# An attention laid out as 64 partitions x 9 tokens, multiplied in 64x64 quadrants, ahead of two expert layers

## The chip, the core and the metric

The kernel runs on one core of one Trainium2 chip. The metric is the device time of one execution in microseconds (us), lower is better; a kernel's time is the median over its runs. A profile is one execution of its own, taken by the hardware profiler, with its own time. Engines: PE is the matrix engine (PEld its weight loads), DVE, ACT and POOL work on tiles, SP issues most DMAs, and 16 DMA engines move the data.

## The reference, cut to what matters

Attention without softmax over 8 batches, 8 heads, 576 tokens and 64 features, a root-mean-square norm per head, then two mixture-of-experts layers over the 4608 tokens. All inputs are fp32.

```python
kv = np.einsum('bhsd,bhse->bhde', k, v)          # 64 x 64 for each batch and head
out = np.einsum('bhsd,bhde->bhse', q, kv)
rms = np.sqrt(np.mean(out * out, axis=-1, keepdims=True) + 1e-06)
x = out / rms * g_norm                           # then rows of 8 heads x 64 = 512, 4608 tokens
# first layer: logits x @ w_gate + log1p(exp(x @ w_noise)) * noise, two best of 8 experts,
#   softmax over the two, sum of relu(x @ w1[e]) @ w2[e]
# second layer: tokens with x @ w_skip > 0 go to the best of 8 experts and are added to
```

## The kernel before

One program, in two phases.

**The attention phase** reads q, k and v, multiplies, normalises, computes the gate logits, and writes rows of 512 features (as two fp16 halves, high and low part, in the bytes of 512 fp32) to `xrows` in HBM, with 16 numbers of routing behind each row. Its work is written out by hand as steps. `subs` (L791) lists 56 of them: for each pair of batches `pb`, 2 x 6 steps of main tokens and 2 of left-over tokens. In step i the loop of L828 runs slot 0 of what is due, transposes the queries of step i+2 (`q_transposed`, L453), runs slot 1, makes the output of step i (`out_sub`, L475), and runs slot 2. Everything else is placed by `at(step, f, slot)`: the tables `KV`, `GC`, `FIN`, `ROUTE`, `WSTEPS`, `EPLAN` and `CLEAR` at the top of the file give the steps. ACT, DVE, POOL and SP take their instructions in just this order (`manual_schedule`, L292), as PE does throughout.

- Loads (L318 to L336). The 576 tokens of a head are 512 main tokens, 4 on each of 128 partitions, and 64 left-over ones. k and v come in half batches (4 heads, 1 KB per partition and head), q in quarters (2 of the 4 tokens of a partition, 512 B runs), the left-over tokens of two batches together (256 B runs).
- Key-value products (`kv_half`, L407): for each head two 128x128x128 products on pairs of tokens (L416), of whose four 64x64 blocks the two on the diagonal are wanted, then one for the left-over tokens of two heads (L421). ACT and DVE add the two blocks (L424, L426), and POOL and ACT copy the sum into both diagonal blocks of `kvbd` (L315 runs what is due), a block-diagonal 128x128 matrix with 32 columns behind it.
- Gate columns (`gate_columns`, L437): key-value times gate weights goes into these 32 columns (L442 to L451), so that the output product gives the logits too.
- Output (`out_sub`): for each head and pair of tokens one 128x160 product with `kvbd` (L481); the left-over tokens use 64-column halves of the array (L487, L488). An eviction (L490 on ACT or L492 on DVE, by the letters of `OSBE`) brings three heads from the bank to `osb`; a square (L495 on ACT, L497 on POOL, by `SQE`) and a sum (L501, DVE) follow a step later.
- `finish` (L504) places, one to six steps later, the inverse root (L517 to L521, L146 to L148), the normalisation (L525, POOL), the logits (L546, L549), the high part (L529, ACT), the low part (L532, DVE) and the write of the rows (`rows_out`, L703, SP).
- `route_half` (L553) chooses the experts of half of the tokens (four batches), mostly on DVE, in 27 pieces; for the first half they are placed between later steps by `ROUTE`, for the second they come in the tail (`TAIL`, L856) together with four early tiles of expert 0 (`early_tile`, L732). In between lie the splitting of expert 0's weights into fp16 halves (L173, L190, L191), and nine DMAs that clear the output (`clear`, L814).

PSUM has 8 banks: pool `pA` 3 (transposes, first expert layer), `pB` 2 (outputs, second layer), `pS` 2 (small), `pK` 1 (key-value).

**The expert phase** (L876 on) gathers rows of `xrows` by expert and runs both expert layers (L232 and L271 are their products). The change leaves it alone, but for the names of the PSUM pools.

## Time and profile before

| | |
|---|---|
| median of 3 runs | 1272.91 us (1269.75 to 1274.32) |
| the profiled execution | 1278.91 us, its span 1276.7 us |
| PE busy | 1184.7 us, 93% of the span |
| DVE, ACT, POOL busy | 823.3, 664.9, 372.5 us (64, 52, 29%) |
| DMA | 293 MB, mean 230 GB/s |

The span runs from the first instruction to the last; times inside it count from its start. A busy share is an average over both phases, which have different limits, so it is read by stretch. Each row of the sections below is a whole line of the profile or of an answer of the trace. In groups of instructions, "out<-in shapes xcount | busy us, mean ns | idle before" gives first the operation and its tiles, then the time in which at least one of them ran, the mean of one, and the engine's idle time just before them with what ended it. "64*128" on PE is rows by columns of the array in use. An fp32 product is recorded as two instructions, an fp32 transpose as one.

### The profile page before, as it was taken

What the parts mean: (1) busy time and instruction counts of PE and PEld (TensorE: products, weight loads), DVE (VectorE), ACT (ScalarE), POOL (GpSimd) and SP (SyncE); (2) the same over time, 40 slices, a digit from 0 to 9 for tenths busy, and PEclk for the clock granted to TensorE, in tenths of its full rate; (3) what the DMA queues carried; (4) which work ended last, traced back from release to release, by engine and by line L of the source; (5) the groups of instructions that cost most, each with busy time, mean ns of one, the idle gap of its engine ahead of it and who ended that gap; (6) DMA issues with size and microseconds to landing.
All of it is one profiled execution on the core that took longest, in us unless ns stands there. A gap on an engine that the chain in (4) does not pass through costs nothing.

```text
span 1276.7 us, 25310 instructions
## 1 busy us (share of the span) xinstructions
PE 1184.7 (93%) x9341; PEld 845.6 (66%) x9341; DVE 823.3 (64%) x3034; ACT 664.9 (52%) x1209; POOL 372.5 (29%) x454
## 2 busy tenths in 40 slices
PE   5868779999999999999999999999899899999996
PEld 5767667767676767676767666676657565666664
DVE  1667887526586877787778877787867665333321
ACT  2578663156664765675667776576754231122210
POOL 2223242202323333324232323233232231312220
PEclk8979789999999999999999999999999999999998
DMA  9999984748996989699799999999995664786570
GB/s 239 291 238 295 320 226 107 180 137 244 297 246 181 232 254 243 190 246 313 132 308 270 289 301 287 255 251 277 276 311 150 141 209 121 221 289 192 155 261 16
DMA packets 311409, 293.33 MB, mean 230 GB/s; under 512 B 205022, under 2 KB 256222, under 8 KB 307180
## 3 DMA queue, kind: packets, MB, share of 16 engines
q1 hardware_dynamic: 288316, 208.22, 62.6%
q0 software_dynamic: 22384, 82.36, 18.7%
q8 instruction: 75, 1.23, 0.4%
q10 hardware_dynamic: 576, 1.05, 0.3%
q14 instruction: 58, 0.48, 0.1%
HBM read 172.86 MB, written 93.42 MB: 209 GB/s over the span
## 4 chain that ended last, share of the span: by engine, by line
PE 62%; issue 12%; DVE 9%; ACT 6%; DMA 6%; POOL 3%; SPq 1%; POOLq 0%; DVEq 0%; ACTq 0%
PE b L271 29%; PE a L232 26%; DMA x2T<-xh 2%; PE b L481 1%; PE kvps L416 1%; ACT wjunk L173 1%; DMA vm<-in_v_dram 1%; DMA x2Tr<-xh 1%; POOL out_dram L1190 1%; DVE xh L933 1%; DMA yo<-ydram,gi 1%; DVE wb L191 1%; ACT wb L190 1%; DVE x L532 1%; PE a L463 1%
## 5 line engine op out<-in xcount | busy, mean ns | idle before, releaser
L232 PEld LDWEIGHTS <-wa 128*128 128x128 f16 x5184 | 460.8, 99 | 52.7 <-issue 4.7
L232 PE MATMUL a<-xT,wa 128*128 128x256 f16 (+6 forms) x3648 | 390.4, 268 | 2.0 <-DMA xT<-xg 1.1
L271 PE MATMUL b<-wb,hh 128*128 128x512 f16 x1488 | 338.8, 380 | 9.9 <-ACT hh L240 9.8
L271 PEld LDWEIGHTS <-hh 128*128 128x128 f16 x1488 | 141.3, 98 | 169.3 <-ACT hh L240 13.9
L240 ACT ACTIVATE hh<-a 128x512 f16<-128x512 f32 (+5 forms) x186 | 107.2, 579 | 199.9 <-PE a L232 193.7
L271 PE MATMUL b<-wb,hl 128*128 128x512 f16 x744 | 176.2, 380 | 0.0
L241 DVE SCALAR_TENSOR_TENSOR hl<-a,hh 128x512 f16<-128x512 f32 (+5 forms) x186 | 124.5, 674 | 72.5 <-ACT hh L240 72.4
L1049 POOL DMA_INDIRECT xg<-xrows,idxp x67 | 65.4, 976 | 320.6 <-DVE orow L1073 279.7
L271 PEld LDWEIGHTS <-hl 128*128 128x128 f16 x744 | 72.9, 98 | 88.6 <-issue 1.1
L1103 ACT ACTIVATE ysb<-b,gate 128x512 f32<-128x512 f32 x73 | 49.7, 681 | 118.5 <-PE b L271 104.4
L232 PE MATMUL a<-x2Tr,wa 128*128 128x256 f16 (+1 forms) x1152 | 107.4, 255 | 1.9 <-DMA x2Tr<-xh 1.9
L1111 POOL DMA_INDIRECT out_dram<-x,oi x67 | 68.2, 1018 | 139.5 <-DVE pi L1019 57.1
L173 ACT ACTIVATE wjunk<-stage 128x1024 bf16<-128x1024 f32 x96 | 101.3, 1055 | 2.1
L191 DVE SCALAR_TENSOR_TENSOR presplit<-stage,wscl,presplit 128x1024 f16<-128x1024 f32 x64 | 80.5, 1278 | 15.8 <-ACT presplit L190 14.9
L1082 POOL DMA_INDIRECT yo<-ydram,gi x67 | 71.2, 1062 | 55.2 <-DMA x2T<-xh 17.7
L190 ACT ACTIVATE presplit<-stage,wscl 128x1024 f16<-128x1024 f32 x64 | 71.2, 1140 | 19.6 <-DVE wscl L183 19.6
L481 PE MATMUL b<-kvbd,qTs 128*128 128x160 f32 x256 | 52.8, 346 | 21.8 <-issue 10.0
L929 ACT ACTIVATE jk<-x 128x512 bf16<-128x512 f32 x67 | 42.1, 629 | 58.3 <-DVE x L1107 57.9
L1107 DVE TENSOR_TENSOR x<-ysb,yo 128x512 f32<-128x512 f32 x67 | 46.3, 691 | 25.2 <-ACT ysb L1103 18.4
L525 POOL TENSOR_TENSOR osb<-osb,rinv 128x1024 f32<-128x1024 f32 (+1 forms) x20 | 37.1, 1854 | 86.9 <-DVE rinv L148 71.3
L932 ACT ACTIVATE xh<-x,x2ss 128x512 f16<-128x512 f32 x67 | 45.4, 714 | 31.7 <-DVE x2ss L139 31.7
L481 PEld LDWEIGHTS b<-kvbd,qTs 128*128 128x128 f32 x256 | 42.6, 219 | 26.5 <-issue 10.9
(356 smaller groups left out, 1534.7 us busy)
## 6 DMA issues: line engine op xcount, KB each, us to landing
stage<-in_moe_w_dram SPq DMA_DIRECT2D x32, 2048.0 KB, 10.9
wsd<-presplit SPq DMA_DIRECT2D x8, 2056.0 KB, 9.3
ydram<-ysb SPq DMA_DIRECT2D x64, 256.0 KB, 7.9
wsd<-presplit SPq DMA_DIRECT2D x8, 2048.0 KB, 7.5
out_dram<-zeros SPq DMA_DIRECT2D x9, 1024.0 KB, 8.2
km<-in_k_dram SPq DMA_DIRECT2D x16, 512.0 KB
vm<-in_v_dram SPq DMA_DIRECT2D x16, 512.0 KB, 8.1
qm<-in_q_dram SPq DMA_DIRECT2D x16, 512.0 KB, 6.8
```

What stands on the lines that cost most here:

```text
L173: A.activation(junk, st[:, F * c:F * c + F], AF.Square, accum_out=acc[:, c:c + 1], **kw)
L190: A.activation(hi[:, d], st[:, d], AF.Copy, scale=sc)
L191: V.scalar_tensor_tensor(lo[:, d], st[:, d], sc, hi[:, d], op0=ALU.mult, op1=ALU.subtract)
L232: PE.matmul(ps[:, i, :], a[:, c, fs], xT[:, b + c, 0:nt], start=(n == 0), stop=(n == 11))
L240: behind[0] = A.activation(hh[:, fsl, 0:nt], ps, AF.Relu).ins
L241: i = V.scalar_tensor_tensor(hl[:, fsl, 0:nt], ps, 0.0, hh[:, fsl, 0:nt], op0=ALU.max, op1=ALU.subtract)
L271: PE.matmul(ps, a[:, f, gsl], b[:, f, :], start=(fs.start == 0 and i == 0), stop=(fs.stop == 8 and a is hl and f == 7))
L481: PE.matmul(po[:, i, :], qT[:, i, :], kvb[b % 4][:, h0 + i, :], start=True, stop=True)
L1049: G.indirect_dma_start(out=xg[:, g], out_offset=None, in_=xrows, in_offset=bass.IndirectOffsetOnAxis(ap=idx[:, t0 + g:t0 + g + 1], axis=0))
L1082: G.indirect_dma_start(out=yo, out_offset=None, in_=ydram[0:BASE[e], :], in_offset=bass.IndirectOffsetOnAxis(ap=gi[:, g:g + 1], axis=0), b ...
L1103: A.activation(ysb, ps, AF.Copy, scale=gate[:, g:g + 1])
L1111: s = G.indirect_dma_start(out=out, out_offset=bass.IndirectOffsetOnAxis(ap=oi[:, g:g + 1], axis=0), in_=x2[:, g], in_offset=None, bounds_ ...
```

## The change

A sequence of 576 tokens is laid out as 64 partitions x 9 tokens, and two heads of it fill the 128 partitions: partition 64c + p, tokens 9p to 9p+8 of head 2h+c. So there are no left-over tokens, and a load of two heads is one stretch of HBM with 2304 bytes to a partition. A pair of batches is the unit (`NP` = 4); k, v and q come in half batches (4 heads) of both batches of the pair.

- Key-value products are 64x64x64 in quadrants: row half by head c, column half by batch bl, 9 tokens added up in PSUM; two banks, one for each c. They come in four parts (`KVAT`) 8 to 5 steps before the pair's first output; `kv_out` evicts them (DVE and ACT), and POOL copies each to the other partition half; no block-diagonal matrix is left.
- Queries are transposed as 128x128 still, for two heads and two neighbouring tokens; after it the partition half is the token.
- Output products are 64x64x80 in quadrants: row half by token, column half by batch; two banks for two tokens. 40 steps (4 pairs x 5 pairs of tokens x 2 halves of the heads); the fifth has one token.
- All evictions are on ACT, all squares on POOL; of the copies of transposed queries 5 in the first 20 are on DVE, the rest on ACT.
- The places of routing, weights, early tiles, clears and finish are set anew for 40 steps.
- PSUM in this phase: 2 banks for transposes, 2 outputs, 2 small, 2 key-value; in the expert phase 3, 2, 2 as before.

The diff, cut to its core:

```diff
+KVAT = (-8, -7, -6, -5)
-CLEAR = (36, 37, 38, 39, 40, 41, 42, 43, 44)
+CLEAR = (17, 19, 21, 23, 25, 27, 29, 31, 33)
-KV, GC = (7, 4), ((3, 2), (1, 2))
-FIN = ((1, 0), (1, 1), (1, 2), (3, 1), (3, 1), (6, 0))
+NT, NP = 9, 4
+FIN = ((1, 1), (1, 2), (2, 0), (3, 1), (3, 2), (5, 0))
-ROUTE = (9, 12, 14, ... 57, 57, 57, 61, 61)
+ROUTE = (3, 4, 5, 6, 7, 9, ... 32, 33, 34, 34)
-QTE = "AAVAAVAVVVAVAVVAVAVVVAVAAVAVVVAAAAAAAAAAAAAAVVAAAAAAAAAA"
-OSBE = "VVVVAVAAAAAVVAAVAAVAVAAAAAVAAAAAAAAAAAAAAVAAAAAAAAAVAAAA"
-SQE = "GGGAAAAAAAAGAAGAAAAAAAAAAAAAAAAAAAAAAAAAAAAAAAAAAAAAAAAA"
+QTE = 5 * "AAAV" + 20 * "A"
+OSBE = 40 * ("AA",)
+SQE = 40 * "G"
-WSTEPS = ((7, 12, 12, 13, 13, 15, 15, 15, 18, 19), (20, 25, 26, 26, 27, 28, 29, 34, 34, 36))
+WSTEPS = ((0, 3, 4, 5, 6, 7, 8, 9, 10, 11), (12, 15, 16, 17, 18, 19, 20, 21, 22, 23))
...
+    def psum_pools(to, a, pair):
+        for name, n in (("a", a), ("b", 2), ("s", 2)) + ((("kv", 2),) if pair else ()):
+            psum[name] = to.enter_context(tc.tile_pool(name="p" + name + str(a), bufs=n, space=bass.MemoryType.PSUM))
...
+        def load(nm, src, pb, hh, bufs):
+            t = ld.tile([P, 2, 2, NT, DH], F32, name=nm + "m", bufs=bufs)
             for bl in range(2):
+                SP.dma_start(t[:, bl].rearrange("p h r d -> p h (r d)"),
+                             src[2 * pb + bl, 4 * hh:4 * hh + 4].rearrange("(h c) (p r) d -> (c p) h (r d)", c=2, r=NT))
+            QT[nm, pb, hh] = t
+        def load_kv(pb, hh):
+            load("k", k, pb, hh, 2)
+            load("v", v, pb, hh, 2)
+        def load_q(pb, hh):
+            load("q", q, pb, hh, 3)
+        load_kv(0, 0)
+        load_kv(0, 1)
+        load_q(0, 0)
...
+        def kv_part(pb, hp):
+            km, vm = QT["k", pb, hp // 2], QT["v", pb, hp // 2]
+            o = hp % 2
+            if hp == 0:
+                kvps[pb] = [psum["kv"].tile([P, 4, DH], F32, name="kvps") for _ in range(2)]
+            for r in range(NT):
+                for bl in range(2):
+                    for c in range(2):
+                        sc, sb = slice(64 * c, 64 * c + 64), slice(64 * bl, 64 * bl + 64)
+                        PE.matmul(kvps[pb][c][sb, hp, :], km[sc, bl, o, r, :], vm[sc, bl, o, r, :],
+                                  start=(hp == 0 and r == 0), stop=(hp == 3 and r == NT - 1), skip_group_check=True)
+        def kv_out(pb):
+            kv = kvb[pb % 2]
+            for c, ps in enumerate(kvps.pop(pb)):
+                for bl in range(2):
+                    sb, so = slice(64 * bl, 64 * bl + 64), slice(64 - 64 * bl, 128 - 64 * bl)
+                    if bl:
+                        A.activation(kv[sb, c::2, bl, 0:DH], ps[sb], AF.Copy)
+                    else:
+                        V.tensor_copy(kv[sb, c::2, bl, 0:DH], ps[sb])
+                    G.tensor_copy(kv[so, c::2, bl, 0:DH], kv[sb, c::2, bl, 0:DH])
...
+        def q_transposed(i):
+            pb, m, hh = subs[i]
+            r = min(2 * m, NT - 2)
+            tp = psum["a"].tile([P, 4, P], F32, name="a")
+            for j in range(4):
+                PE.transpose(tp[:, j, :], QT["q", pb, hh][:, j // 2, j % 2, r:r + 2, :], ident)
+            qT = wk.tile([P, 4, P], F32, name="qTs", bufs=3)
...
+        def out_sub(i, qT, osb):
+            cs = range(2) if 2 * m + 1 < NT else (1,)
+            po = {c: psum["b"].tile([P, 4, DH + 16], F32, name="b") for c in cs}
+            for j in range(4):
+                for c in cs:
+                    for bl in range(2):
+                        sc, sb = slice(64 * c, 64 * c + 64), slice(64 * bl, 64 * bl + 64)
+                        PE.matmul(po[c][sb, j, :], qT[sc, 2 * bl + j // 2, 64 * (j % 2):64 * (j % 2) + 64], kv[sc, 4 * hh + j, bl, :],
+                                  start=True, stop=True)
+            for t, c in enumerate(cs):
+                if OSBE[i][t] == "A":
+                    A.activation(osb[:, t, hs], po[c], AF.Copy)
...
+            def rows_out():
+                t0 = 1 + NT * P * pb
+                SP.dma_start(xrows[t0:t0 + NT * P, 0:512].rearrange("(p r) w -> p r w", r=NT)[:, 2 * m:2 * m + n],
+                             x16[:, 0:n].rearrange("p t w -> p (t w)").bitcast(F32).rearrange("p (t w) -> p t w", w=512))
...
+        subs = [(pb, m, hh) for pb in range(NP) for m in range(5) for hh in range(2)]
+        FIRST = -8
+        for pb in range(NP):
+            s0 = 10 * pb
+            for hp in range(4):
+                step = s0 + KVAT[hp]
+                at(step, kv_part, pb, hp)
+                if hp % 2 and pb + 1 < NP:
+                    at(step + 1, load_kv, pb + 1, hp // 2, slot=0)
+            if pb == 0:
+                at(-6, load_q, 0, 1, slot=0)
+                at(-3, load_q, 1, 0, slot=0)
+            if pb + 1 < NP:
+                at(s0 + 7, load_q, pb + 1, 1, slot=0)
+            if pb + 2 < NP:
+                at(s0 + 8, load_q, pb + 2, 0, slot=0)
+            g = gate_columns(pb)
+            at(s0 - 4, kv_out, pb, slot=2)
+            for d in (3, 2):
+                at(s0 - d, next, g, None, slot=2)
+        at(FIRST, gate_weights)
```

## Rows read from the trace of the kernel before

**Rows 1.** Windows: stretch, length, busy us (instructions) per engine, clock, DMA share, GB/s

```profile
28.40:199.50 171.10, 133.98 (x1021) 121.94 (x1022) 126.75 (x310) 116.47 (x260) 53.61 (x43) 0.86 0.95 268
199.50:241.00 41.50, 39.41 (x442) 27.75 (x442) 30.44 (x90) 10.73 (x23) 14.29 (x24) 1.00 0.44 108
241.00:1276.70 1035.70, 996.90 (x7799) 682.97 (x7799) 663.47 (x2625) 532.41 (x915) 296.00 (x351) 0.99 0.81 228
```

**Rows 2.** Chain that ended last, 0 to 260 us: start, length, engine, tile, line

```profile
28.45 1.05 PE b L481 x6
...
199.53 0.45 ACT osb L490
...
204.00 0.64 DVE na L576
...
241.04 10.64 PE a L232 x96
```

**Rows 3.** Waits of PE, 28.4 to 199.5: us in total, times, longest

```profile
PE b L481 <- issue: 10.0, 3, 3.8
PE small L442 <- DVE sw L426: 7.0, 5, 4.0
PE b L481 <- POOL kvbd L315: 6.6, 2, 4.2
```

**Rows 4.** Timeline, 42.7 to 43.6 us: start, length, instruction [idle before]

```profile
42.80 0.54 ACT L451 ACTIVATE kvbd<-small 64x128 f32<-64x128 f32 x2
...
43.44 0.61 PE L481 MATMUL b<-kvbd,qTs 128*128 128x160 f32 x1 [3.84 <-issue]
```

**Rows 5.** Groups of instructions by form, 0 to 204 us: PE

```profile
L481 PE MATMUL b<-kvbd,qTs 128*128 128x160 f32 x256 | 52.8, 346 | 21.8 <-issue 10.0 <-POOL kvbd L315 6.6 <-POOL rhs L665 1.5
...
L416 PE MATMUL kvps<-vm,km 128*128 128x128 f32 x256 | 39.9, 322 | 12.9 <-DMA vm<-in_v_dram 11.8 <-DVE sw L426 1.1
...
L463 PE MATMUL a<-ident,qm 128*128 128x128 f32 x128 | 26.5, 318 | 0.0
```

**Rows 6.** Timeline of PE, 58.45 to 59.4 us, neighbours of one line merged

```profile
58.28 0.27 PE L463 MATMUL a<-ident,qm 128*128 128x128 f32 x1
58.48 0.45 PE L487 MATMUL b<-kvbd,qTs 128*64 128x128 f32 x4
...
58.84 0.44 PE L487 MATMUL b<-kvbd,qTs 128*64 128x128 f32 x4
...
59.30 0.33 PE L463 MATMUL a<-ident,qm 128*128 128x128 f32 x1
```

**Rows 7.** Groups by form, 0 to 204 us: ACT

```profile
L495 ACT ACTIVATE sq<-osb 128x384 f32<-128x384 f32 x29 | 15.2, 523 | 6.4 <-DVE osb L492 5.0 <-DVE rmsa L146 0.5
L490 ACT ACTIVATE osb<-b 128x480 f32<-128x480 f32 x25 | 14.1, 564 | 4.4 <-PE b L481 4.3
...
L466 ACT ACTIVATE qTs<-a 128x384 f32<-128x384 f32 x24 | 11.4, 481 | 2.6 <-PE a L463 2.5
...
L495 ACT ACTIVATE sq<-osb 128x256 f32<-128x256 f32 x22 | 9.2, 417 | 4.8 <-DVE osb L492 4.2
...
L490 ACT ACTIVATE osb<-b 128x320 f32<-128x320 f32 x18 | 7.7, 430 | 2.3 <-PE b L488 2.2
```

**Rows 8.** Groups by form, 0 to 204 us: DVE and POOL

```profile
L525 POOL TENSOR_TENSOR osb<-osb,rinv 128x1024 f32<-128x1024 f32 x16 | 32.8, 2047 | 72.3 <-DVE rinv L148 62.8 <-DVE zt L546 9.5
...
L501 DVE TENSOR_REDUCE ss<-sq 128x6 f32<-128x384 f32 x32 | 17.4, 546 | 7.9 <-ACT sq L495 5.9 <-POOL sq L497 1.9
...
L497 POOL TENSOR_TENSOR sq<-osb 128x384 f32<-128x384 f32 x3 | 2.6, 861 | 8.9 <-ACT osb L490 5.5 <-DVE osb L492 3.4
```

**Rows 9.** DMA view, 47:49 (256 B), 134:136 (512 B), 129:130 (1 KB), 97:99 (2 KB)

```profile
DMA packets 1553, 0.39 MB, mean 195 GB/s; under 512 B 1545, under 2 KB 1553, under 8 KB 1553
...
DMA packets 1142, 0.59 MB, mean 293 GB/s; under 512 B 1, under 2 KB 1141, under 8 KB 1142
...
DMA packets 379, 0.38 MB, mean 382 GB/s; under 512 B 6, under 2 KB 379, under 8 KB 379
...
DMA packets 379, 0.78 MB, mean 388 GB/s; under 512 B 0, under 2 KB 0, under 8 KB 379
```

325 lines of the change are left out of this document (97 added, 228 removed).

## The prediction, made before the changed kernel was run

> **What bounds the kernel now.** I read the windows first, cut at the landmarks of the chain: the first product of a query (28.45), the last eviction of the attention (199.53), the start of the second routing half (204.00), the first group of the expert phase (241.04) [rows 2]. The expert phase, 1035.7 us with PE at 997, is not touched by the change. The tail between 199.5 and 241.0 is one chain (finish, routing on DVE, gather, transpose) with the early expert tiles beside it; its instructions stay what they are. So the change is worth what it takes off the stretch 28.4 to 199.5, the 56 steps of the attention.
>
> In that stretch no compute engine is full: PE 134.0 of 171.1 us, DVE 126.8, ACT 116.5, POOL 53.6, and the granted clock is 0.86, between its levels of 1.2 and 2.4 GHz; DMA has the highest share, 0.95 [rows 1]. But PE hardly waits for a DMA there. Its longest waits, some 24 us in all, come where a batch's key-value product is handed over [rows 3]: the 3.84 us marked "issue" before 43.44 is such a one, because the ACT copy of the gate columns, the last thing that the next product reads, ends at 43.34 [rows 4]; it stood in ACT's order behind work that itself waited for DVE. So four engines in fixed orders hold each other up, PE the fullest at 134.0/171.1 = 78%. The stretch gets shorter if the fullest engines get less work and fewer hand-overs, down to what the loads allow.
>
> **The change part by part.**
>
> *Key-value and output products (PE).* Before, a 128x160 fp32 product is two records of 206 ns (52.8 us/256), a 128x128 one two of 156 ns (39.9/256); a transpose costs 207 ns (26.5/128) [rows 5]. After, there are 576 products of 64x64x64 for key-value and 576 of 64x64x80 for the output, in fours that use the four quadrants, and 160 transposes. That two column halves do run side by side is seen: the products of the left-over tokens (128 rows by 64 columns, 128+32 moving columns) start a second head 0.36 us after the first, with both halves of a head inside that time [rows 6], against 2 x 0.41 us for two such products in sequence [rows 5]. No row shows two row halves at once. Between four at once and two at once I take four, because two halves already run as separate streams: a four then costs half of a 128-column product or of a 160-column one, 144 x 156 ns = 22 us and 144 x 206 ns = 30 us; transposes 160 x 207 ns = 33 us; gate products, as now, an estimate of 10 us. Sum 95 us against 134. Two at once: 44 + 59 + 33 + 10 = 146 us. One at a time: 90 + 119 + 33 + 10 = 252 us.
>
> Mode switches: the rows show no idle time where a transpose (58.28, recorded for 0.27 us) is followed by the 64-column products (58.48), nor on the way back [rows 6]. The Trainium skill, page TensorEngine Tiling (Array Packing), section Tiling Modes, says that a change of tiling mode drains the TensorE; this change switches twice in each of its 40 steps and twice around each of 16 key-value parts, 112 times. What such drains would give is a rival below.
>
> *ACT.* All squares leave it: 15.2 + 9.2 = -24.4 us. Evictions: now 72 of 128x320, all on ACT, 72 x 0.430 = 31.0 us against 14.1 + 7.7 = 21.8: +9.2. Transposed queries: 35 copies of 512 columns, 0.481 x 4/3 = 0.64 us, 22.4 against some 16: +6.7. The small copies around a batch's key-value tile (mostly 256 columns, an estimate of 0.430 x 256/320 = 0.34 us) fall from 56 to 16: -13.8 [rows 7]. 116.5 - 22.3 = 94 us.
>
> *DVE.* Sums of squares keep their elements (32 x 0.546 x 4/3 + 8 x 0.36 = 26 us, as now [rows 8]); it loses 13 evictions, 14 of 19 query copies and 16 additions and gets 16 small copies, net 27 instructions at the 0.43 to 0.56 us that ACT pays for such shapes [rows 7]: -14. Low-part subtraction, logits, weights and the first routing half stay. 126.8 - 14 = 113 us. DVE becomes the fullest.
>
> *POOL.* Normalising stays (32.8 us and its small forms). All squares come here: 32 x 0.861 x 4/3 + 8 x 0.57 = 41 us [rows 8], some 4 of it there already; the copies of the key-value tile to the other half stay 16. 53.6 + 37 = 91 us. The sum of squares now waits for POOL, where a square can stand behind a 2.05 us normalisation; queued behind that wait on DVE are the query's and the routing's instructions, but the sum is issued a step later, so a step of 2.05 + 1.15 = 3.2 us hides it.
>
> *Loads.* 28.3 MB in stretches of 2304 bytes in place of 16.8 MB in 1 KB, 8.4 MB in 512 B and 3.1 MB in 256 B. The rows give 382, 293 and 195 GB/s for these and 388 for 2 KB [rows 9]: 44 + 29 + 16 = 89 us become 28.3/0.385 = 73.5 us. That is 15 us off the DMA rings, which nobody waits for now, so nothing on the path by itself. But the loads keep a ceiling: a fourth query tile may be loaded only when the first is used up, two steps before its own use. Counted from 4 us at 385 GB/s, all that is queued up to q of the second pair's second half (18.9 MB of loads, 2 MB of weights, some 3 us of small ones) has landed near 62 us, when step 9 needs it. At 3.6 us a step, step 9 comes at 61; at 2.6 us it would come at 52 and wait 10. The clears (9 x 1 MB, 3.4 us each by the 512 B row) move ahead of the last query loads, one in two steps; they fit into 7 us of step time.
>
> *Start and moved edits.* The first pair needs 5.9 MB before its first output, 15.3 us from 4 us on, then products, copies and gate columns of about 8 us, as now: first product again near 28. Taken at no cost: the memsets and iotas that go, at the head of POOL's and DVE's orders while the first loads are under way. The gate weights' scaling moves to the head of DVE's order and waits there for a load that stands behind 5.9 MB, until about 20 us; queued behind it is the first key-value copy, due at 22. Steps of routing, weights and early tiles are placed anew on 40 steps; the first routing half (about 20 us of DVE) falls on 12 steps, which DVE's sum already has.
>
> **The sum.** The fullest engine held 78% of the stretch; DVE at 113 us and the same share gives 113/0.78 = 145 us, last eviction at 28.4 + 145 = 173 in place of 199.5: -26. There are four hand-overs in place of eight, each with one more step of slack before its use, which gives back half of the 24 us of PE waits at most; I count 2 of it, since a DVE-bound stretch covers most. -28 us. The profiled execution took 1278.9 us (span 1276.7 and 2.2 around it): 1251. The median of the runs shown is 6.0 below it, so 1272.9 - 28 = **1245 us**.
>
> **The rivals.**
> - *Pace set by the loads alone.* DVE at 95% would end at 28.4 + 119 = 147; the wait of about 10 us for the query tile brings it to 157. -43: 1230 us. For it: DVE's waits for ACT and PE shrink with their work. Against: the first routing half still ties DVE, PE and ACT together.
> - *Drains at each mode switch.* 112 switches at a transpose's recorded 0.27 us are 30 us: PE 95 + 30 = 125, the fullest again; 125/0.78 = 160, last eviction at 189, -11: 1262 us. The rule named above would give this one; the rows of the two switches speak against it.
> - *Row halves don't run at once.* PE 146 us, at 78 to 90% of the stretch 187 to 162 us, last eviction at 215 to 190: +16 to -9, 1264 to 1289 us; middle 1275. It decides from 134 us of PE work upward (slower). For it: no row shows two row halves together. Against: two column halves are.
> - *Output banks taken in pairs (slower).* A step now takes both buffers of the output pool, where it took one. If PE's next outputs wait for both ACT copies and ACT for PE in turn, a step is PE's and ACT's work in sequence: 95/40 + 94/40 = 4.7 us, 40 of them 189 us, last eviction at 217, +18: 1291 us. It decides at 171.1/40 = 4.28 us a step. Against it: transposes two steps ahead and the other ACT work lie between.
>
> **How the numbers follow.** Differences under 0.5% (6.4 us) can't be told from no change here. Forecast 0.57 (1236 to 1256), loads alone 0.18, drains 0.09, row halves 0.10, output banks 0.06. Faster by over 0.5%, that is under 1266.5: the first two and most of the third, 0.57 + 0.18 + 0.07 = 0.82; same: the rest of the third and 0.04 of the fourth, 0.06; slower: 0.06 of the fourth and the last, 0.12. The range runs from 1224, a little under the loads' case, since its 10 us of wait may be less, to 1268, past the drains and the better end of the row halves; it leaves out 0.12 above and some 0.05 at the ends.
>
> **What would show it.** Right: four 64x64 products starting within a quarter of a microsecond; PE busy near 95 to 110 us up to the last eviction, ACT near 94 and DVE near 113; that eviction at 165 to 180; then again some 41 us to the first expert group and 1036 us behind it. Wrong: PE records of the quadrants in sequence (row halves); idle PE between a transpose and quadrants (drains); waits of PE for q (loads); PE waiting for evictions in each step (banks); or a tail that gives the gain back.

## The result and the profile after

The changed kernel takes 1287.41 us (median of four runs, 1286.35 to 1291.68), the kernel before, run beside it, 1273.62. The ratio is 1.0118, 95% interval 1.0083 to 1.0153: slower by about 14 us. The forecast was 1245 us, so it had the wrong sign and missed by 42 us.

First the windows of the profile after, cut at the landmarks of [rows 1], but at the end of the last eviction, where [rows 1] cuts at its start, 0.45 us earlier; the columns are those of that group.

```profile
33.10:204.60 171.50, 122.50 (x2564) 102.51 (x2564) 122.18 (x260) 89.74 (x203) 93.68 (x75) 0.69 0.72 238
204.60:249.00 44.40, 41.02 (x442) 28.14 (x441) 31.46 (x89) 10.04 (x22) 15.40 (x25) 0.96 0.44 112
249.00:1284.50 1035.50, 995.03 (x7799) 682.49 (x7799) 664.76 (x2631) 532.80 (x915) 295.08 (x351) 0.99 0.79 229
```

The stretch from the first output to the last eviction is as long as before, 171.5 us, although ACT fell from 116 to 90 us and PE from 134 to 123. It begins 4.6 us later, and the tail behind it is 44.3 us in place of 41.1 (ends of the last eviction, 204.65 and 199.97, to the first expert group, 248.96 and 241.04). The expert phase is the same in the two profiles. DMA, at 0.95 before, is at 0.72.

So the landmarks place 7.9 of the 14 us. The rest lies in no stretch of these two profiles: the profiled execution of the kernel before took over 5 us more than its median, that of the changed kernel was the shortest of its four.

The step that matters most was not taken in the prediction: cutting the stretch at the start of the first routing half (the first `na`, 122.5 us before and 123.1 after). First the kernel before, then the changed one:

```profile
28.45:122.50 94.05, 74.17 (x523) 68.18 (x524) 62.48 (x155) 64.80 (x139) 25.64 (x23) 0.87 1.02 285
122.50:200.00 77.50, 60.31 (x503) 53.95 (x502) 64.72 (x157) 52.06 (x123) 28.47 (x20) 0.85 0.86 244
```

```profile
33.10:123.10 90.00, 68.28 (x1541) 57.01 (x1540) 55.10 (x123) 51.38 (x113) 45.43 (x39) 0.70 0.84 300
123.10:204.60 81.50, 54.22 (x1023) 45.50 (x1024) 67.09 (x138) 38.35 (x90) 48.25 (x37) 0.69 0.60 171
```

DVE, 74% busy over the whole stretch before, is 66% busy in the first part and 84% in the second (64.72 of 77.5). DVE's busy time falls by 7.4 us in the first part and grows by 2.4 in the second. The first part gets 4 us shorter, the second 4 us longer.

The groups of instructions, 28 to 205 us, that answer to [rows 5, 7, 8]: PE, ACT, POOL and DVE.

```profile
L446 PE MATMUL b<-kvb,qTs 64*64 64x80 f32 x1152 | 48.6, 295 | 18.7 <-ACT osb L451 13.8 <-issue 4.6
L429 PE MATMUL a<-ident,qm 128*128 128x128 f32 x156 | 35.9, 369 | 3.0 <-DVE qTs L434 2.1 <-DMA qm<-in_q_dram 0.9
L385 PE MATMUL kvps<-vm,km 64*64 64x64 f32 x864 | 20.5, 252 | 7.8 <-issue 7.8
L417 PE MATMUL kvps<-gw,kvT 64*64 64x16 f32 x240 | 13.5, 264 | 0.0
...
L451 ACT ACTIVATE osb<-b 128x320 f32<-128x320 f32 x72 | 27.7, 432 | 24.9 <-PE b L446 24.6
L432 ACT ACTIVATE qTs<-a 128x512 f32<-128x512 f32 x34 | 20.2, 593 | 11.5 <-PE a L429 11.4
...
L460 POOL TENSOR_TENSOR sq<-osb 128x512 f32<-128x512 f32 x32 | 36.6, 1149 | 40.4 <-ACT osb L451 35.8 <-DVE gt L581 3.7 <-DVE ss L464 0.9
...
L464 DVE TENSOR_REDUCE ss<-sq 128x8 f32<-128x512 f32 x32 | 21.7, 679 | 21.9 <-POOL sq L460 21.9
```

No engine waits for one other engine throughout. But one wait of PE has no semaphore behind it ("issue"), and it comes in the middle of a run of equal products. The timeline of PE, 40 to 43.6 us:

```profile
39.81 0.63 PE L385 MATMUL kvps<-vm,km 64*64 64x64 f32 x27
43.30 0.60 PE L385 MATMUL kvps<-vm,km 64*64 64x64 f32 x12 [2.86 <-issue]
```

The DMA view shows what is under way then: in 40.43 to 41.80 us one packet of the instruction queue beside the loads, and in 41.80 to 43.30 none. The same view over 28 to 205 us shows such packets, 16 KB each, first before, then after (queue: packets, MB, share):

```profile
q8 instruction: 1, 0.02, 4.7%
```

```profile
q8 instruction: 9, 0.15, 0.3%
```

```profile
q8 instruction: 21, 0.34, 0.8%
```

So between 28 and 205 us the changed kernel fetches 21 blocks of PE instructions in place of 9, because a 64x64 product is as many instructions as a 128x128 one and there are more of them (2564 records of products and transposes in the stretch in place of 1023). There are five such stops over half a microsecond (0.70 at 18.4, 2.86 at 40.4, 4.38 at 50.4, 3.34 at 91.3, 1.61 at 132.2), 12.9 us in all. The kernel before has none: its "issue" waits [rows 3, 4] are at instructions that wait for a semaphore, and none is near a packet. The five stops lie at the 222nd, 604th, 859th, 1496th and 2134th record of a product or transpose (an fp32 product has two), which lie multiples of about 127.5 apart, or 255 instructions, since each has a weight load of its own. In each of the five, PE goes on 1.3 to 1.6 us after a block has landed. Loads fill the DMA engines at the first four (share 1.00 to 1.05), not at the last (0.23); the block's packet takes 0.9 to 1.1 us at all five. The Trainium skill, page Runtime: NRT & Kernel Launch, section Instruction fetch mechanics, says that instructions come in blocks of 16 KiB, 256 of them, and that crossing a block's end is "mostly hidden". The first agrees with this trace (16 KB packets, stops at multiples of 255 instructions); the second doesn't hold at these five places.

### The profile page after: what moved, and what is told of

Read it like the earlier page. It is cut to its first block, busy times and chain, and to the rows that moved or that the text cites. A ratio compares the mean times of both kernels' runs of the same rounds, so it can differ in the third digit from the quotient of the medians.

```text
span 1284.5 us, 28856 instructions
## 1 busy us (share of the span) xinstructions
PE 1175.7 (92%) x11181; PEld 828.0 (64%) x11181; DVE 820.8 (64%) x2989; ACT 636.6 (50%) x1145; POOL 408.0 (32%) x479
## 3 DMA queue, kind: packets, MB, share of 16 engines
q10 hardware_dynamic: 576, 1.05, 0.3%
## 4 chain that ended last, share of the span: by engine, by line
PE 57%; issue 15%; DVE 10%; DMA 6%; ACT 5%; POOL 5%; SPq 1%; POOLq 0%; DVEq 0%; ACTq 0%
PE b L273 28%; PE a L234 25%; DMA qm<-in_q_dram 2%; DMA x2T<-xh 1%; ACT wjunk L175 1%; DVE x L494 1%; POOL out_dram L1135 1%; POOL osb L485 1%; DVE wb L193 1%; DVE xh L878 1%; PE b L446 1%; DVE ss L464 1%; DMA yo<-ydram,gi 1%; ACT wb L192 1%; POOL x2r L1105 1%
## 5 line engine op out<-in xcount | busy, mean ns | idle before, releaser
L234 PEld LDWEIGHTS <-wa 128*128 128x128 f16 x5184 | 461.0, 99 | 55.2 <-issue 7.0
L234 PE MATMUL a<-xT,wa 128*128 128x256 f16 (+6 forms) x3648 | 389.2, 267 | 1.7 <-DVE hl L243 1.3
L273 PE MATMUL b<-wb,hh 128*128 128x512 f16 x1488 | 337.4, 379 | 8.8 <-ACT hh L242 8.7
L273 PEld LDWEIGHTS <-hh 128*128 128x128 f16 x1488 | 141.2, 98 | 167.5 <-ACT hh L242 12.5
L273 PE MATMUL b<-wb,hl 128*128 128x512 f16 x744 | 175.8, 379 | 0.0
L273 PEld LDWEIGHTS <-hl 128*128 128x128 f16 x744 | 72.7, 98 | 87.8 <-DVE hl L243 0.3
L234 PE MATMUL a<-x2Tr,wa 128*128 128x256 f16 (+1 forms) x1152 | 109.0, 257 | 3.9 <-DMA x2Tr<-xh 3.9
L874 ACT ACTIVATE jk<-x 128x512 bf16<-128x512 f32 x67 | 42.2, 629 | 57.8 <-DVE x L1052 57.4
L446 PE MATMUL b<-kvb,qTs 64*64 64x80 f32 x1152 | 48.6, 295 | 18.7 <-ACT osb L451 13.8
L446 PEld LDWEIGHTS b<-kvb,qTs 64*64 64x64 f32 x1152 | 39.5, 181 | 28.7 <-ACT osb L451 18.8
L460 POOL TENSOR_TENSOR sq<-osb 128x512 f32<-128x512 f32 (+1 forms) x40 | 43.6, 1094 | 44.2 <-ACT osb L451 39.6
```

The source lines that it names most:

```text
L234: PE.matmul(ps[:, i, :], a[:, c, fs], xT[:, b + c, 0:nt], start=(n == 0), stop=(n == 11))
L273: PE.matmul(ps, a[:, f, gsl], b[:, f, :], start=(fs.start == 0 and i == 0), stop=(fs.stop == 8 and a is hl and f == 7))
L446: PE.matmul(po[c][sb, j, :], qT[sc, 2 * bl + j // 2, 64 * (j % 2):64 * (j % 2) + 64], kv[sc, 4 * hh + j, bl, :], start=True, stop=True)
```

## The experiments

All ratios are to the kernel before in the same session. Landmarks come from the one profile of each run, in us from its start: the first output, the start of the first routing half, the last eviction, the start of the expert phase; then the busy time of PE, DVE, ACT and POOL between the first output and the last eviction.

| run | ratio (95%) | output | routing | eviction | experts | PE, DVE, ACT, POOL |
|---|---|---|---|---|---|---|
| before | 1 | 28.5 | 122.5 | 200.0 | 241.0 | 134, 127, 117, 54 |
| after | 1.0118 (1.0083 to 1.0153) | 33.1 | 123.1 | 204.6 | 249.0 | 123, 122, 90, 94 |
| e1 | 1.0045 (1.0017 to 1.0073) | 33.1 | 122.3 | 202.6 | 244.8 | 124, 114, 112, 49 |
| e2 | 1.0072 (1.0037 to 1.0107) | 35.3 | 124.1 | 206.8 | 249.0 | 122, 123, 90, 94 |
| e3 | 1.0094 (1.0066 to 1.0121) | 33.1 | 123.5 | 206.0 | 250.9 | 138, 122, 91, 93 |
| e4 | 1.0078 (1.0038 to 1.0117) | 30.1 | 125.0 | 211.1 | 252.1 | 140, 139, 94, 100 |
| e5 | 1.0048 (1.0026 to 1.0070) | 32.2 | 121.0 | 203.7 | 247.7 | 124, 123, 90, 93 |
| e6 | 1.0023 (0.9998 to 1.0048) | 33.1 | 117.6 | 199.1 | 243.9 | 122, 123, 90, 94 |
| e8 | 1.0032 (1.0011 to 1.0052) | 32.4 | 117.3 | 196.7 | 239.3 | 124, 114, 112, 49 |
| e9 | 1.0056 (1.0035 to 1.0077) | 32.1 | 118.4 | 199.3 | 243.8 | 125, 117, 101, 71 |
| e10 | 1.0155 (1.0127 to 1.0182) | 33.0 | 129.5 | 218.6 | 264.5 | 125, 143, 90, 97 |
| e11 | 1.0100 (1.0072 to 1.0128) | 34.9 | 123.2 | 205.1 | 252.1 | 131, 123, 90, 95 |
| e12 | 0.9992 (0.9963 to 1.0021) | 32.2 | 116.7 | 197.5 | 241.9 | 119, 111, 107, 70 |
| e13 | 1.0030 (1.0003 to 1.0057) | 31.8 | 117.3 | 196.5 | 239.0 | 121, 107, 118, 50 |
| e14 | 1.0073 (1.0045 to 1.0101) | 33.1 | 120.2 | 203.0 | 245.3 | 124, 123, 90, 94 |
| e15 | 0.9975 (0.9950 to 0.9999) | 31.6 | 116.4 | 195.7 | 240.0 | 126, 112, 108, 71 |
| e16 | 1.0197 (1.0150 to 1.0243) | 33.0 | 181.1 | 179.0 | 262.6 | 112, 99, 88, 82 |
| e17 | 1.0009 (0.9983 to 1.0035) | 31.6 | 121.7 | 194.8 | 237.2 | 121, 112, 108, 71 |
| e18 | 0.9991 (0.9964 to 1.0017) | 31.7 | 121.4 | 193.5 | 235.7 | 116, 109, 112, 60 |

The expert phase, the same work in all, takes 1026 to 1045 us in these profiles, so single profiles are compared by landmarks up to its start, and whole kernels by the ratios. Between sessions the ratios agree to about half a per cent only: e3, whose landmarks are 2 us worse than those of the changed kernel, has a ratio 0.0024 lower. So a gain over the changed kernel is read from the landmarks first.

### Squares and banks (e1, e3, e4)

Two theories stood first: squares on POOL put POOL into the chain of every step (theory P), or taking both output banks in a step ties PE to ACT's evictions (theory B, a rival of the prediction).

**e1**, the changed kernel with its squares on ACT:

```diff
-SQE = 40 * "G"
+SQE = 40 * "A"
```

> The changed kernel with all 40 squares on ACT again, nothing else. Theory P (the squares made POOL a link of every step: sum of squares on DVE waits for POOL 22.7 us, POOL waits for evictions 39.6 us, a square stands behind a 2.05 us normalisation): DVE's wait for POOL goes, DVE runs faster beside an idler POOL, the stretch up to the last eviction falls by 15 to 30 us, the time to 1258 to 1272 us. Theory B (the two output banks, both taken by a step, tie PE to the ACT evictions): ACT gets 40 x 0.65 = 26 us more work ahead of its next evictions, PE waits longer, the time is 1287 to 1300 us.

The last eviction comes 2.0 us earlier and the tail is 2.2 us shorter; by the ratios it would be about 9 us. That is less than theory P said, and against theory B. DVE's busy time falls by 8 us, though DVE does the same work. Two of its small operations in the changed kernel and then in e1 (groups, 28 to 205 us):

```profile
L477 DVE TENSOR_SCALAR vv<-ss 128x8 f32<-128x8 f32 x3 | 1.9, 644 | 0.1
...
L144 DVE SCALAR_TENSOR_TENSOR rmsa<-rinv 128x16 f32<-128x16 f32 x16 | 4.6, 289 | 3.1 <-ACT rinv L481 3.1
```

```profile
L477 DVE TENSOR_SCALAR vv<-ss 128x8 f32<-128x8 f32 x4 | 1.4, 357 | 0.1
...
L144 DVE SCALAR_TENSOR_TENSOR rmsa<-rinv 128x16 f32<-128x16 f32 x16 | 2.8, 173 | 8.4 <-ACT rinv L481 8.4
```

The 16 instructions of L144 take 289 ns in place of 173. In the trace of the changed kernel, 11 of them that run while POOL is idle take 166 ns on average, and 5 that start while a POOL instruction runs 561; each of the 5 ends 0.03 us behind that POOL instruction. The subtraction of L494 takes 1.21 us, but 2.10 where it starts just behind a square on POOL (timeline, 92.3 to 94.7 us):

```profile
92.46 1.04 POOL L460 TENSOR_TENSOR sq<-osb 128x512 f32<-128x512 f32 x1 [0.82 <-ACT osb L451]
92.48 2.10 DVE L494 TENSOR_TENSOR x<-osb,x 128x1024 f16<-128x1024 f32 x1
```

Where L494 starts first, POOL's instruction takes longer: a copy (L397) 1.43 us in place of 0.40, a square 1.43 and 1.53 in place of 1.04. The sums of squares (L464), beside POOL or not, take 0.68 us. So it is a class of DVE's instructions, not all of them, that POOL holds up and that holds POOL up, whichever starts first. The Trainium skill, page SBUF — State Buffer, section SBUF: two separate sides, describes a pair of ports shared by DVE and POOL, locked for a whole instruction, and names operations with two SBUF inputs among those that need it. L144 and L494, both with two SBUF inputs, agree with it.

**e3**, the changed kernel with the output products of one bank first, then those of the other:

```diff
-            for j in range(4):
-                for c in cs:
+            for c in cs:
+                for j in range(4):
```

> The changed kernel with the output products of a step in the order token by token (one bank filled, then the other), in place of head by head. Two quadrants work at a time in place of four, but the first bank is free for ACT half a step earlier. Theory B: the evictions start earlier and PE waits less for ACT (13.8 us now): 6 to 15 us off, 1272 to 1281 us. Theory P: within 4 us of 1287, or longer by what the halved number of quadrants costs, 40 x 0.3 = 12 us at most.

PE's wait for ACT's evictions falls from 13.8 to 8.2 us, and still there is no gain: the last eviction is 1.4 us later, with PE 15 us busier. With e1, where ACT has more to do ahead of its evictions and the time falls, theory B falls.

**e4**, the kernel before with all its squares on POOL:

```diff
-SQE = "GGGAAAAAAAAGAAGAAAAAAAAAAAAAAAAAAAAAAAAAAAAAAAAAAAAAAAAA"
+SQE = 56 * "G"
```

> The kernel before with all 56 squares on POOL (5 are there already), nothing else. Theory P: the same link arises in the old layout, the time rises by 8 to 25 us, to 1281 to 1298. Theory B: ACT loses 24 us of work, its evictions come earlier, the time falls by 0 to 8 us.

In the old layout the same step costs 10 us (the expert phase starts 11.1 us later), with DVE 11 us busier. So some 4 us (landmarks of e1) to 10 us (e4) of the result belong to where the squares are made, not to the layout.

### The start (e2, e5)

The changed kernel's first output comes at 33.10 in place of 28.45 [rows 2]. Its chain, 20 to 40 us:

```profile
23.57 8.01 DMA qm<-in_q_dram
...
31.63 1.54 PE a L429 x6
33.17 1.28 PE b L446 x32
```

PE transposes queries two steps ahead and works in order, so the first output waits for the second query tile, which is loaded behind the next pair's keys.

**e2** loads that tile earlier (`load_q(0, 1)` right behind `load_q(0, 0)`, and not at step -6).

> The changed kernel with the second query tile of the first pair loaded right behind the first one, ahead of the second pair's keys and values. Its first output came at 33.1 us in place of 28.4, behind a query load that landed at 31.6. Both theories: the first output comes at 28 to 30 us; 3 to 5 us off the time if the steps behind it keep their pace, 0 to 2 if they wait later for the loads that were pushed back.

The first output comes later, at 35.3. The chain, 4 to 34 us, shows why:

```profile
14.09 11.19 DMA gw<-in_moe_w_noise_dram
...
25.41 0.28 DVE gw L355
25.69 0.34 DVE kvb L397
```

The gate weights, now behind 1.2 MB more, land at 25.3; DVE's scaling of them stands at the head of its order and holds the key-value copies, the very hold-up that the prediction had put at no cost with the loads as they are.

**e5** loads the gate weights first as well.

> The changed kernel with the gate weights loaded first and the first pair's second query tile loaded right behind its first one, ahead of the second pair's keys and values. Theory S (start): the first product at 33.1 us in place of 28.5 is a wait for this query tile, because the queries are transposed two steps ahead and PE takes its orders in sequence; the first product then comes at 27 to 29 us, and 4 to 5 us of the 14 come back. Rival: the second pair's keys and values land 3 us later, the batch's hand-over waits for them instead, and the last eviction stays at 204 to 206 us, the time at 1285 to 1289.

The first output is still at 32.2, 0.9 us earlier in place of 4 to 5. No query is on the way to the first output any more; PE's own work is on the chain of 10 to 36 us:

```profile
18.94 3.96 PE kvps L386 x138
...
26.85 3.53 PE kvps L418 x64
30.38 1.90 PE a L430 x8
32.28 1.28 PE b L447 x32
```

The last values land at 18.8 and the first output comes 13.5 us later. In the kernel before it came 6.4 us after the last load (22.02 to 28.45). The gate columns alone are 64 records and 3.5 us, for a pair of batches, in place of 8 and 1.0 for the first batch.

### The instruction blocks (e6, e7)

**e6** cuts every key-value part in two and lays the halves of the last two pairs on eight steps (some of the next pair's loads move by one step with them):

```diff
-KVAT = (-8, -7, -6, -5)
+HALVES = [(-8, -8, -7, -7, -6, -6, -5, -5), (-8, -7, -7, -6, -6, -5, -5, -4)] + 2 * [(-11, -10, -9, -8, -7, -6, -5, -4)]
...
-            for r in range(NT):
+            for r in rs:
```

> The changed kernel with each key-value part cut in two (5 and 4 of the 9 tokens), and for the last two pairs the eight halves laid on eight steps instead of four. Nothing else moves. Theory C (instruction blocks): the small products need 21 blocks of 16 KB of PE instructions in the stretch in place of 9; PE uses one up in 2 us within a key-value part and then stands in mid-part, without a semaphore, until the next block has come over the same DMA engines as the loads: 12.9 us in five stops. Spread, the stops in the last two pairs (3.3 and 1.6 us) go, those of the second pair get shorter, and 4 to 8 us come back. Rival: PE has 48 us of idle time in the stretch, the stops only replace other waits; they go, and the time stays within 2 us.

The stops fall from 12.9 to 5.2 us, the expert phase starts 5.0 us earlier, and against the kernel before the ratio is 1.0023, an interval that touches 1. The halves of the stretch say where:

```profile
33.10:117.60 84.50, 68.19 (x1613) 57.62 (x1612) 55.39 (x122) 52.01 (x113) 45.11 (x39) 0.73 0.87 313
117.60:199.10 81.50, 53.33 (x951) 44.61 (x952) 67.11 (x138) 38.36 (x90) 48.62 (x37) 0.69 0.61 177
```

The first part loses 5.5 us; its stops fell by 5.4 (from 10.6, those at 40, 50 and 91 us, to 5.2). The second part keeps its 81.5 us to the decimal, though its stop of 1.61 is gone too. So here a stop counts in full in the first part and not at all in the second. Runs that change nothing ahead of the routing bear out the first half of this: in e14 the three stops are 2.6 us shorter together and the first part 2.9 us, in e16 1.8 us, and its 38th eviction, the last ahead of the routing, comes 1.6 us earlier. They also show that these stops differ by some 2 us between profiles of the same instructions, and the changed kernel's profile has the longest, so the 5.5 us of e6 are rather its upper end.

**e7** adds a one-column product behind each key-value product.

> The changed kernel with a second product of a single moving column behind each of the 576 key-value products (it adds to the first column of the key-value tile, so the values differ). It adds 9 blocks of PE instructions to the 21 and little streaming. Theory C: stops of PE without a semaphore grow from 12.9 to 25 us or more, nearly all at multiples of a block, and the time grows by 6 to 15 us. Rival (PE has slack for both): the stops may grow, PE is busy some 10 to 19 us longer, and the time grows by less than 4 us.

Up to the last eviction the blocks rise from 23 to 32 and the stops from 12.9 to 20.5 us, less than theory C said; the first output comes 9 us later and the last eviction 26, more than either theory expected. PE's busy time rises by 26 us as well, so this run does not separate the fetches from the products' own time; e6 does. Its expert phase, with other values to route, is not comparable (16137 us in all).

### Which engine sets the pace (e10, e11)

**e10** does the low-part subtraction on DVE twice, **e11** every query transpose on PE twice.

```diff
                 V.tensor_tensor(lo, xv, hi, op=ALU.subtract)
+                V.tensor_tensor(lo, xv, hi, op=ALU.subtract)
```

> The changed kernel with the low-part subtraction on DVE done twice (20 more of 1.1 us, 22 us of DVE work in the stretch, same values). By the rule of the prediction, that the stretch is the fullest engine's work over 0.78, it would grow by 28 us. Theory D: DVE is the bound only from the start of the first routing half at 123 us on; the start of that half stays within 2 us of 123, and the last eviction comes 9 to 13 us later, for the ten that lie behind it. Rival: hops between engines set the pace everywhere and DVE's idle time takes the work up: less than 4 us.

> The changed kernel with every query transpose done twice (160 more, some 35 us of PE work at the mixed clock, one block of instructions more, same values). If PE is the bound or each PE hop lies on the path, the last eviction comes 20 to 35 us later. Theory H (no engine is full; a part of the PE hops lies on the path, and more work may raise PE's clock): 5 to 15 us, with the granted clock in the stretch above 0.69. Rival (PE's idle time of 48 us takes it): under 4 us.

Doubling on DVE makes it 20.9 us busier, and the last eviction comes 14.0 us later, half of what the prediction's rule gives: 6.4 us in the first part for 11.6 of work, 7.6 in the second for 9.4. So theory D, which allowed 2 us in the first part and put 9 to 13 behind it, is only half right: DVE's work counts in the first part too, with 0.55 us for each us, and in the second with 0.81. Doubling on PE changes nothing up to the last eviction (+0.5), and PE is only 8 us busier for 160 transposes more. The window of e11 from first output to last eviction:

```profile
34.90:205.10 170.20, 130.52 (x2715) 112.67 (x2715) 122.77 (x260) 89.95 (x203) 94.50 (x75) 0.79 0.73 236
```

The granted clock is 0.79 in place of 0.69, so PE does more work in nearly the same time. PE's 134 us before and 123 after were therefore no amounts of work that a time could be scaled with. And since 8 us more of PE's time here and 15 in e3 move the last eviction by 0.5 and 1.4 us, PE's time is not the bound of the changed kernel.

### The second part (e14, e16)

In the second part PE waits in its order for pieces of the routing (waits of PE, 123 to 206 us):

```profile
PE b L446 <- ACT osb L451: 11.3, 7, 3.5
PE small L623 <- DVE vv L477: 5.2, 1, 5.2
PE small L573 <- DVE m L566: 4.7, 1, 4.7
PE small L623 <- DVE ohp L614: 3.0, 2, 2.4
```

**e14** moves pieces of the first routing half alone, so that PE's part of it comes later than what it reads:

```diff
-ROUTE = (3, 4, 5, 6, 7, 9, 10, 11, 12, 14, 15, 16, 18, 19, 20, 22, 23, 24, 26, 27, 29, 30, 31, 32, 33, 34, 34)
+ROUTE = (3, 4, 5, 6, 7, 8, 9, 10, 11, 12, 13, 14, 15, 16, 20, 21, 22, 23, 24, 25, 28, 30, 32, 34, 36, 37, 38)
```

> The changed kernel with the places of the first routing half's pieces alone moved: the pieces up to the choice of the second expert closer together, the rank products four slots (1.3 steps) behind the sum they read in place of one, the six one-hot pieces two slots apart, the end one step later. Theory R (PE stands in its order for the routing): three waits of 4.7, 5.2 and 3.0 us of PE for DVE in this half fall below 5 us together, the outputs behind them come earlier, the last eviction at 196 to 201 in place of 204.6, the time 1280 to 1284. Rival (DVE is the bound in this half, PE's waits only show its idle time): the last eviction stays at 203 to 206, since DVE's work is the same.

These three waits fall from 12.9 to 1.9 us, with 3.9 for POOL, 2.4 for another result of DVE and 2.0 more for a later sum in their place. The last eviction comes 1.6 us earlier, on the rival's side of the line, and none of that lies in the second part, which takes 82.8 us in place of 81.5. PE's waits showed its idle time, not the cause.

**e16** puts the whole first routing half behind the last output (`ROUTE = 27 * (61,)`, and the first slots and the early tiles' first pieces behind it).

> The changed kernel with the whole first routing half, the first slots and the early tiles' first pieces put behind the last output (before the second routing half), so that this half of the attention runs without routing; the work itself stays, and the tail grows by it. Read is the last eviction, not the total. Theory D (the second half of the attention is paced by DVE's routing, some 20 us, beside its other work): the last eviction falls from 204.6 by 8 to 16 us. Rival (the steps keep a pace of about 4.1 us by their own chain over PE, ACT, DVE and POOL): it falls by less than 4 us. In both cases the start of the expert phase comes later than 249.

DVE has 22.8 us less to do, and the last eviction comes 25.6 us earlier, more than theory D said. The parts, cut behind the 38th of the 72 evictions, the last ahead of the routing in the changed kernel (where it ends at 118.3 us):

```profile
33.00:117.00 84.00, 65.90 (x1445) 54.91 (x1448) 51.55 (x115) 49.98 (x110) 43.51 (x38) 0.68 0.84 300
117.00:179.00 62.00, 45.76 (x972) 37.44 (x969) 47.80 (x91) 38.31 (x88) 38.84 (x32) 0.72 0.75 233
```

Behind that eviction the attention takes 62.3 us in place of 86.3. So the second part is paced by DVE with the routing on it, here by 1.1 us for each us of DVE's work. PE and POOL have 11 us less to do as well, but more work on PE (e3, e11) and 21 us less on POOL in this part (e1) move it by 1 us or so. The price of DVE's work is not the same everywhere: e1 takes 4.3 us of it from the second part, where POOL no longer holds DVE up, and gives ACT 10 us more; the part gets 1.2 us shorter. As the tail gets all that work back, the total is worse.

### Versions of the changed layout (e8, e9, e12, e13, e15, e17, e18)

**e8** joins e5, e6 and squares on ACT. 

> The changed kernel with the three together: gate weights and first queries loaded ahead, key-value parts spread, all squares on ACT. If start (4.5 us), instruction stops (4 to 8) and squares on POOL (7) are separate causes that add up, 1287 becomes 1268 to 1272, at or under the kernel before. If they hide each other, it stays at 1275 to 1281, near the version with the squares on ACT alone.

 Up to the expert phase the causes nearly add up: it starts at 239.3, 9.7 us earlier than in the changed kernel (1.3, 5.0 and 4.2 in e5, e6 and e1) and 1.7 us earlier than in the kernel before. The total, 1.0032, doesn't show it.

**e9** is e8 with every second step's squares on POOL (`SQE = 20 * "AG"`). 

> The version with early queries, spread key-value parts and squares on ACT, but with every second step's squares on POOL: ACT falls from 111 to about 101 us in the stretch, POOL rises from 49 to about 71, DVE stays near 114 to 118. Theory of the in-order chain (no engine is full, each step's hop over ACT counts): the shorter ACT order is worth 2 to 5 us, 1274 to 1277. Rival (what POOL takes from DVE costs as much): no change, 1278 to 1281.

 There is no gain, as the rival said; the expert phase even starts 4.5 us later than in e8.

**e12** and **e13** give DVE's copies out of PSUM to ACT, with squares as in e9 and as in e8. 

> The version with early queries, spread key-value parts and every second step's squares on POOL, with DVE's copies out of PSUM (five transposed queries, the key-value and gate copies) given to ACT: DVE falls from 117 to about 109 us in the stretch, ACT rises from 101 to about 111. If DVE's work counts with the slope that its doubling showed (14.0 us for 20.9 us of work, 0.67), the last eviction comes 5 us earlier than in that version, at 194, and the ratio to the kernel before falls by 0.004. Rival (ACT, now as full, takes its place): the last eviction stays at 198 to 201.

 

> The same with all squares on ACT: DVE about 106 us, ACT about 121, POOL 49. With DVE's slope and nothing lost on ACT the last eviction, 196.7 with DVE at 114, comes at 191 to 192. If ACT, the fullest engine now beside PE, has a slope as large as DVE's, the two cancel and it stays at 196 to 199.

 DVE falls by 7 us in each, 5.2 and 5.4 of them in the first part, and the last eviction comes 1.8 and 0.2 us earlier: near the rival, work given from DVE to ACT gives little or nothing. (The ratios of e9 and e12, of two sessions, would say more.)

**e15** is e12 with the routing of e14. 

> The same move in the version with early queries, spread key-value parts, half of the squares on POOL and DVE's copies on ACT, where these waits are 5.3, 5.2 and 6.7 us and the last eviction is at 197.5. Theory R: last eviction at 188 to 194, ratio to the kernel before 0.992 to 0.997. Rival: 196 to 199 and 0.998 to 1.001.

 The last eviction comes 1.8 us earlier, as in e14, between the two forecasts and next to the rival's. At 0.9975 (0.9950 to 0.9999) it is the best version, and less than can be told from no change.

**e17** is e15 with the second weight matrix split at steps 15 to 18, ahead of the routing, **e18** that with the squares of the last 20 steps on ACT. 

> The version of the last but one run (early queries, spread key-value parts, half of the squares on POOL, DVE's copies on ACT, routing with slack), with the second weight matrix split at steps 15 to 18 in place of 15 to 23, so that its last four low parts (1.28 us each, 5 us of DVE) lie ahead of the first routing half. Theory D (the second half is paced by DVE, slope about 1.1 as the removal of the routing showed: 25.6 us for 22.9): start of the routing half to last eviction 73 to 76 in place of 79.3, at a cost of 1 to 3 us ahead of it; last eviction 191 to 194, ratio 0.993 to 0.997. Rival: the first half pays as much as the second gains; 195 to 197.

 

> The same with all squares of the last 20 steps on ACT, which has idle time there, so that POOL's squares neither delay DVE's sums nor lengthen its small instructions. Theory D and the squares' price add: a further 1 to 3 us, last eviction 189 to 193, ratio 0.991 to 0.996. Rival: ACT's order, which feeds PE, gives it back; no change from the run before.

 In e17 the second part falls from 79.3 to 73.1 us, as theory D says, with 3.3 us less on DVE and 3.5 less on ACT in it, and the first grows by 5.3, more than was allowed for it. Neither run reaches the ratio that was expected of it. The halves of e18:

```profile
31.70:121.40 89.70, 66.78 (x1613) 55.71 (x1612) 51.27 (x113) 66.12 (x140) 31.62 (x28) 0.76 0.88 315
121.40:193.50 72.10, 49.61 (x951) 41.04 (x952) 57.90 (x135) 46.04 (x108) 28.70 (x19) 0.76 0.67 186
```

The expert phase starts at 235.7, 5.3 us ahead of the kernel before, but the kernel is no faster within the interval (0.9991). So the layout, with the start, the bursts, the squares, DVE's copies, the routing's places and the weights all moved, comes out even.

## Why the prediction was wrong

**The step that failed** is the first line of its sum: "The fullest engine held 78% of the stretch; DVE at 113 us and the same share gives 113/0.78 = 145 us". e10 refutes the rule as such: 20.9 us more on DVE cost 14.0 us, where the rule gives 27. The 78% was PE's share, over a stretch with two parts that have different limits, and in the changed kernel e3 and e11 show that PE sets the pace of neither. DVE was the fullest in the second part: 64.7 of 77.5 us before, and 47.7 of the first 54.5 of them. The work that the change takes from DVE lay ahead of it: 11 of the 13 evictions and 17 of the 19 query copies, 14.3 of 16.4 us, belong to the first 31 of the 56 steps. So the second part got nothing from it. It even grew by 4 us, of which the squares on POOL explain 1.2 (e1), and where 26 us were forecast, the stretch stayed the same. The sentence on the first routing half, "which DVE's sum already has", is the same error: a sum over the stretch does not say that 20 us of it fall on 12 steps that DVE already fills. e16 shows it for the changed kernel by removal: 25.6 us. That the same part of the kernel before has the same limit is read from its busy shares; no run tests it.

**Not in the sum at all:** instruction fetches. 10.6 us of stops in the first part ate into what the change gained there; where e6 shortened them by 5.4 us, the part got 5.5 us shorter. With e6 the first part is 84.5 us against 94.1 before, so a gain was there, about a third of the 26. What the other 5.2 us of stops cost is not shown.

**DVE's term** was 113 us and measured 122. With the squares off POOL (e1) it is 114: the sum of its instructions was right, and some 8 us are instructions held up by POOL. POOL's own 91 us (93.7 measured) and ACT's 94 (89.7) were about right.

**PE's term** was 95 us and measured 122.5. Four quadrants do run at once: 36 key-value products (72 records) take 1.28 us at the higher level of the clock, 0.14 us for four, a little under the 0.156 forecast. The 432 of them in the stretch took 20.5 us, all 576 28.9 where 22 were forecast. The output products took 48.6 us in place of 30, in large part since the granted clock fell from 0.86 to 0.69: a step's 32 records take 0.73 to 1.10 us at the higher level and 1.34 to 1.66 at the lower, and about half of the records ran at the lower, where it was a fifth of the output products' before. Gate columns and their transposes took 13.5 + 5.4 us in place of 10, and 12.6 us of early tiles, routing and sums (L234, L623, L273, L182) had been left out, though the 134 us contained such work. (Groups overlap, so they add up to more than PE's busy time.) By e3 and e11 PE's time was not what counted.

**The start** was put at no change, with "products, copies and gate columns of about 8 us, as now", and it cost 4.6 us. As now was 6.4 us from the last load, and it became 13.5 (e5): 4 us of products, the granted clock 0.57, copies one after the other on POOL, gate columns in 64 records. In the changed kernel itself the wait for the second query tile hides this.

**The tail**, put at no change, grew by 3.2 us (41.1 to 44.3). With squares on ACT in the last steps it is 42.2 to 42.6 (e1, e8, e13, e18), so some 2 us of it are the last squares on POOL.

**The loads** were right. The first part moves 300 GB/s with stretches at 395 to 405, a little over the 385 taken, and behind the first output PE waits 0.9 us for queries; DMA's share fell and nobody gained by it, as the prediction said of the path. The rival of the loads alone did not come in.

**The rivals**: row halves do run at once (above), and drains are not to be seen where a 128x128 transpose is followed by quadrants and these by transposes [rows 6] (timeline of PE, 33 to 35.2 us):

```profile
32.75 0.42 PE L429 MATMUL a<-ident,qm 128*128 128x128 f32 x1
33.10 1.35 PE L446 MATMUL b<-kvb,qTs 64*64 64x80 f32 x32
34.38 1.11 PE L429 MATMUL a<-ident,qm 128*128 128x128 f32 x4
```
Output banks in pairs, the rival that ended slower, gave 1291 us and was near the result, but its mechanism is refuted: PE waits for ACT's evictions 10 times in 40 steps (13.8 us), e3 made that wait shorter and gained nothing, and e1, with ACT's order longer by 22 us, was faster. It was a right number for a wrong reason.

**What stays open.** No run shows what paces the first part once the stops are gone: in e6 no engine is over 81% there and DMA is at 0.87, and work moved into it costs time (5.3 us in e17) though each engine has room. Nor is it shown why DVE's work costs from 0.3 us (e1, second part) to 1.1 us (e16) for each us. And why the last landmark's gain of e8 and e18 does not show in their totals, and where the 6 of the 14 us of the result lie that no landmark shows, was not tried.

## What to carry to other kernels

Cut the stretch where its work changes before dividing by a busy share, and ask of each removed instruction in which part it lies; an engine that is 74% busy overall can be the bound of one half. Smaller products mean more instructions: count the blocks of PE instructions that a burst uses up, and spread bursts over steps (here 36 products, 144 instructions, in 1.3 us). Doubling one engine's work, without changing values, is a cheap way to learn whose time counts.

## What was not expected of the hardware

- PE stopped five times, for 0.7 to 4.4 us, without a semaphore, mostly in the middle of equal products, until 1.3 to 1.6 us after a 16 KB instruction block had landed; the block's own packet took 0.9 to 1.1 us, at a DMA share of 1.0 as at 0.23.
- 160 more transposes made PE 8 us busier in the stretch, not 36 (an estimate: 160 at the 0.23 us that one took before, 35.9 us for 156): the granted clock rose from 0.69 to 0.79.
- A DVE instruction on 16 elements took 166 ns alone and 561 when it started beside one of POOL's, and a POOL copy 1.43 us in place of 0.40 when it started beside a subtraction on DVE; a sum of 512 elements took 0.68 us either way.
